# Moving the flags of rows without a matching key from VectorE to GpSimd

## The chip, the cores and the metric

One core of a Trainium2 chip runs the whole program. A core has five engines with a queue each: TensorE (PE, with its weight loads as PEld), VectorE (DVE), ScalarE (ACT), GpSimd (POOL) and SyncE (SP), which issues most of the DMA transfers. An engine takes its instructions in the order in which the program issues them, and waits on semaphores for what other engines produce. The metric is the device time of one execution in microseconds; lower is better. TensorE's granted clock is full speed in the whole profile.

## The reference

Bucketed attention over 2 x 8 heads, 768 positions and 64 dimensions, followed by two dense layers with gates. Only the first part matters here:

```python
q_bucket, k_bucket = ...            # 6 sign bits of a projection, as a number
mask = q_bucket[:, :, :, None] == k_bucket[:, :, None, :]
scores = scale * np.matmul(q, k.transpose(0, 1, 3, 2))
scores = np.where(mask, scores, -1000000000.0)
scores = scores - np.max(scores, axis=-1, keepdims=True)
attn = np.exp(scores)
attn = attn / (np.sum(attn, axis=-1, keepdims=True) + 1e-09)
return np.matmul(attn, v).astype(np.float32)
```

A query whose bucket holds no key has all its scores at -1e9; after the maximum is subtracted they are all 0, and its attention is 1/768 for every key. These rows need a flag.

## The kernel before, in words

The attention works on 8 pairs of heads (`NPAIR`), and on each pair in 12 units: one head, 128 queries, all 768 keys. So there are 96 units, numbered 0 to 95. Scores are made with their sign turned, and a large constant is added where the buckets differ: with `BIG` = 2^30, a masked score is at least `BIG / 2`. The softmax's maximum is therefore a minimum here, and a row without a matching key is one whose minimum is at least `BIG / 2`.

A unit n goes through these steps:

- `emit_S` (TensorE, L742): four passes into PSUM: high part of keys by high part of queries, high by low, low by high (`KL`, "kl"), and the bucket bits (`BK`, `BQ`).
- `emit_min` (VectorE, L751): the minimum of each row, into slot 0 of the group's statistics tile "st".
- `emit_exp` (ScalarE, L756): the exponential into tile "p", with the row's sum into slot 1.
- `emit_stats` (VectorE, L764 to L767): for a group of up to four units at once, four small operations that make the factor (slot 3) and the summand (slot 4) of each row.
- `emit_norm` (GpSimd, L772): p times factor plus summand, in place, one instruction for each unit.
- `emit_T` and `emit_tevac`: twelve transposes on TensorE (L784), then copies of the transposed halves out of PSUM into "pt" by ScalarE (L496) and VectorE (L497).
- `emit_pv` (TensorE, L797): attention times values.

The order is written out by hand. `attention_step(n)` takes units n and n + 1 together (n is even) and issues, beside their scores, minima and exponentials, the transposes of units n - 7 and n - 6 and the products of units n - 12 and n - 11. Groups are units 0 to 2, 3 to 6, 7 to 10, and so on to 91 to 94, and 95 alone. From n = 14 on, a step with n % 4 == 2 ends with `stats_norms` for units n - 3 to n: the four statistics on VectorE, then four normalisations on GpSimd.

In the same steps the next pair is prepared (`prep`, by s = (n // 2) % 6). At s = 1 GpSimd makes the high parts of keys and queries (`prep_kh`, `prep_qh`, L500), and, for the fourth pair on, the scaled bits (`prep_scale`, L526). At s = 5 it makes the low part of the keys (`prep_k_lo`, L549), and SyncE then issues the loads of the pair after that (L464, L473), into the buffer that the low part was read from. Both are issued ahead of the step's `stats_norms`:

```python
if nxt and s == 1:
    prep(nxt, s)
if live and n % 4 == 2 and n > 10:
    if nxt and s == 5:
        prep(nxt, s)
    stats_norms(range(n - 3, n + 1))
```

The first two pairs have an order of their own (`late_prep`, `mid_prep`): statistics of units 0 to 2 come after step 4, those of units 3 to 6 after step 6. VectorE and ScalarE also prepare the weights of the dense layers during the attention (`w_slot`, `w_parts`, for instance L155, L164, L147). After the last step the rest is written out: transposes of the last units, statistics and normalisation of unit 95, products, and the first dense matmuls (`emit_h`, L295; `emit_y`, L348). From there to the end, some 530 us, the dense layers run.

Of the kernel before, what the change touches and what calls it, by code (L numbers as in the profile page):

```python
# [8 lines left out]
F32 = mybir.dt.float32  # L9
# [3 lines left out]
ALU = mybir.AluOpType  # L13
AX = mybir.AxisListType
BIG = float(2 ** 30)
# [5 lines left out]
def bucket_attention_two_moe_kernel(  # L21
# [17 lines left out]
    B, H, D, S = q.shape  # L39
# [38 lines left out]
    V, A, G, P = nc.vector, nc.scalar, nc.gpsimd, nc.tensor  # L78
# [35 lines left out]
    units = [(k, i) for k in range(2 * NF) for i in range(2)]  # L114
# [156 lines left out]
    with tc.manual_schedule():  # L271
# [164 lines left out]
        with ExitStack() as actx:  # L436
# [8 lines left out]
            def big2(nm):  # L445
                return [big.tile([128, 2, HALF], F32R, name=f"{nm}{i}") for i in range(2)]

            KH, KL, BK = big2("kh"), big2("kl"), big2("bk")
# [62 lines left out]
            def prep_kh(p):  # L511
                scaled(KH[p % 2], raw_t[p, "k"], 1.0)
# [121 lines left out]
            for h in range(2):  # L634
                G.tensor_scalar(out=BK[1][:, h], in0=BK[1][:, h].bitcast(F32), scalar1=c8[:, 5 + 2 * h:6 + 2 * h],
                                scalar2=1.0, op0=ALU.add, op1=ALU.mult)
# [17 lines left out]
            def first_bq(out, ps, less):  # L654
                V.tensor_scalar(out=out, in0=ps, scalar1=0.0, scalar2=less, op0=ALU.is_gt, op1=ALU.subtract)
# [29 lines left out]

            first_z = []

            def mid_prep(n):
                if n == 2:
                    first_z.append(z_all("t1", q0[0][:, halves[1]], odd=q0[1][:, halves[1]]))  # L690

            def late_prep(n):
                if n == 0:
                    first_bk(1, "t1")
                    first_bq(bx[:, halves[0]], z_all("t0", q0[1][:, halves[0]]), cvec0)
                    first_q(1, 1)
                elif n == 2:
                    first_bq(BQ[0][:, halves[1]], first_z.pop(), cvec0)
                    prep_kh(1)
                    prep_qh(1)  # L700
                    rest_of(QL[1][0][:, halves[0]], raw_t[1, "q"][:, halves[0]].bitcast(F32),
                            QH[1][0][:, halves[0]], halves[0])
                    swap(QL[1], halves[0])
                elif n == 4:
                    prep_bit(1)
                    prep_scale(1)
                    stats_norms(range(3))
                    prep_bits(1, (0, 1, 3))
                elif n == 6:
                    load_v(0)  # L710
                    emit_stats(1, range(3, 7))
                    for x in (3, 4, 5):
                        emit_norm(x)
                    prep_k_lo(1, 0)
                    emit_norm(6)
                    prep_k_lo(1, 1)
                    G.tensor_scalar(out=BK[0][:, 1], in0=BK[1][:, 1].bitcast(F32), scalar1=1.0, scalar2=1.0,
                                    op0=ALU.mult, op1=ALU.mult)


            L = 7
            NU = NPAIR * 12
            s_t, p_t, st_t, pt_t, tb_t, pv_t = {}, {}, {}, {}, {}, {}
# [34 lines left out]
                p_t[n] = pt  # L758


            def emit_stats(b, units):
                mine = slice(units[0] + 1 - 4 * b, units[-1] + 2 - 4 * b)
                least, total, inv, mul, add = (st_t[b][:, i, mine] for i in range(5))
                V.tensor_scalar(out=add, in0=least, scalar1=BIG / 2, scalar2=1.0 / S, op0=ALU.is_ge, op1=ALU.mult)  # L764
                V.tensor_scalar(out=inv, in0=total, scalar1=1e-9, scalar2=None, op0=ALU.add)
                V.reciprocal(out=inv, in_=inv)
                V.scalar_tensor_tensor(out=mul, in0=least, scalar=BIG / 2, in1=inv, op0=ALU.is_lt, op1=ALU.mult)  # L767

            def emit_norm(n):
                b, i = divmod(n + 1, 4)  # L770
                st = st_t[b]
                G.tensor_scalar(out=p_t[n], in0=p_t[n], scalar1=st[:, 3, i:i + 1], scalar2=st[:, 4, i:i + 1],  # L772
                                op0=ALU.mult, op1=ALU.add)
# [38 lines left out]
            def emit_pv_hi(gi):  # L812
                for hi, lo, src in x_parts(gi):
                    A.copy(hi, src)
# [6 lines left out]


            def stats_norms(units):
                emit_stats((units[0] + 1) // 4, units)
                for n in units:
                    emit_norm(n)

            def attention_step(n, w_act=(), w_dve=(), mid=lambda: None, between=lambda: None):
                u = n - L
                m = n - 12  # L830
                live = n < NU
                have = [0 <= u + k < NU for k in range(2)]
                if n == NU:
                    stats_norms(range(NU - 1, NU))
                def first_T():
                    if have[0]:
                        emit_T(u)
                        emit_tevac(u, 0, acp)
                        if n < 14:
                            emit_min(n)  # L840
                        emit_tevac(u, 1, acp if live and n >= 14 else vcp)
                        if n == 12:
                            stats_norms(range(7, 11))

                if n >= 14:
                    first_T()
                if n == 0:
                    for i, passes in ((0, range(3)), (1, range(1)), (0, range(3, 4)), (1, range(1, 4))):
                        emit_S(i, passes)
                elif live:  # L850
                    emit_S(n)
                    if n < 14:
                        first_T()
                    emit_S(n + 1)
                mid()
                if have[1]:
                    emit_T(u + 1)
                s = n // 2 % 6
                nxt = n // 12 + 1 if live and n // 12 + 1 < NPAIR else None
                if nxt and s == (2 if nxt < 3 else 1):  # L860
                    prep_z(nxt)
                for k in (m, m + 1):
                    if 0 <= k < NU:
                        emit_pv(k // 6, k % 6)
                out_gi = m // 6 if m + 2 == NU else m // 6 - 1 if m >= 6 and m % 6 == 0 else None
                if out_gi is not None:
                    emit_pv_hi(out_gi)
                    if live and out_gi % 2 == 0:
                        out_gi = None
                if live and s == 4 and m > 0:  # L870
                    out_gi = m // 6 - 1
                for part in w_act:
                    part()
                early = live and have[1]
                if early and n >= 14:
                    emit_tevac(u + 1, 0, acp)
                if live:
                    if n >= 14 or not have[0]:
                        emit_min(n)
                    emit_exp(n)  # L880
                    emit_min(n + 1)
                if early and n < 14:
                    emit_tevac(u + 1, 0, acp)
                between()
                if have[1]:
                    emit_tevac(u + 1, 1, acp if n == 6 else vcp)
                if have[1] and not early:
                    emit_tevac(u + 1, 0, acp)
                if n + 2 < NU:
                    emit_exp(n + 1)  # L890
                if n == 12:
                    prep_q_lo(1, 1)
                    swap(QL[1], halves[1])
# [6 lines that stand above are left out]
                elif nxt and s == 5:  # L900
                    prep(nxt, s)
                if nxt and s not in (1, 5):
                    prep(nxt, s)
                if out_gi is not None:
                    emit_pv_lo(out_gi)
                    if out_gi % 2 == 1 and out_gi // 2 + 2 < NPAIR:
                        load_v(out_gi // 2 + 2)
                for part in w_dve:
                    part()
# [15 lines left out]
            for n in range(0, NU, 2):  # L925
                if n == 12:
                    two_banks()
                attention_step(n, *w_at.get(n // 2, ((), ())),
                               mid=lambda: mid_prep(n))
# [16 lines left out]
            def late_pv(gi):  # L946
                for j in range(NJ):
                    emit_pv(gi, j)
# [8 lines left out]
            emit_exp(NU - 1)  # L957
            late_T(NU - 6, "s0")
            late_pv(last - 1)
            stats_norms(range(NU - 1, NU))  # L960
            late_out(last - 2)
            qctx.close()
            more = ctx.enter_context(tc.tile_pool(name="more", bufs=1, reuse_waits="tile"))
# [75 lines left out]
```

## Time and profile before

| | |
|---|---|
| median of 3 runs | 729.79 us (729.0 to 729.97) |
| profiled execution | 729.23 us, its span 727.5 us |
| TensorE busy | 721.1 us (99%), 4726 matmuls |
| VectorE busy | 483.1 us (66%), 908 instructions |
| ScalarE busy | 422.9 us (58%), 808 instructions |
| GpSimd busy | 136.0 us (19%), 139 instructions |
| attention stage, about | 0 to 197 us |

Times in the trace count from the start of the span. A busy share is an average over stages: GpSimd works only in the attention stage, and there it is busy for most of the time. An instruction's idle time is put down to what released it; where several semaphores are waited for, to the one that came last.

### The profile page before, as it was taken

The page shows a single profiled execution, that of the slowest core. Times are in us where ns is not written, and L with a number is a line of the kernel's source. Part 1 is how long each engine was busy: PE and PEld are TensorE (multiplying, and loading weights), DVE is VectorE, ACT ScalarE, POOL GpSimd, SP SyncE. Part 2 cuts the span into 40 slices and gives each one's busy share as a digit, 9 for nine tenths or more (in the row PEclk, how much of TensorE's full clock was granted, in tenths as well). Part 3 has the DMA queues.
Part 4 walks back from the last instruction along what each step waited for, and adds up shares of the span by engine and source line. Part 5 has one row for each costly group of instructions (what it writes and reads, how often), then busy time and mean ns, then how long its engine had stood idle before and what let it go on. Part 6 is the DMA issues. An engine that isn't in the chain of part 4 may idle for free.

```text
span 727.5 us, 12377 instructions
## 1 busy us (share of the span) xinstructions
PE 721.1 (99%) x4726; PEld 571.8 (79%) x4726; DVE 483.1 (66%) x908; ACT 422.9 (58%) x808; POOL 136.0 (19%) x139
## 2 busy tenths in 40 slices
PE   8999999999999999999999999999999999999998
PEld 5776776767778888888888888888888888888886
DVE  8989889888899969696582386584665556121212
ACT  6898888889787857674462264553444444222221
POOL 6876676665500000000000000000000000000000
PEclk9999999999999999999999999999999999999999
DMA  4433434341043322232120002122112100010101
GB/s 137 147 120 85 138 109 126 101 147 65 2 145 117 124 108 89 85 117 75 41 87 29 1 29 84 37 83 84 62 58 81 64 30 1 0 59 1 58 1 58
DMA packets 20274, 54.29 MB, mean 75 GB/s; under 512 B 3008, under 2 KB 7032, under 8 KB 20216
## 3 DMA queue, kind: packets, MB, share of 16 engines
q1 hardware_dynamic: 19912, 53.28, 22.1%
q8 instruction: 37, 0.61, 0.3%
q10 hardware_dynamic: 304, 0.23, 0.1%
q14 instruction: 21, 0.17, 0.1%
HBM read 43.39 MB, written 3.15 MB: 64 GB/s over the span
## 4 chain that ended last, share of the span: by engine, by line
PE 98%; DVE 2%; ACT 0%; issue 0%; DVEq 0%
PE s L348 34%; PE t L295 18%; PE pv L295 10%; PE s L742 9%; PE m L295 7%; PE t L784 5%; PE pv L797 5%; PE m L797 5%; DVE st L751 1%; PE m L348 1%; PE m L486 1%; PE t L348 1%; PE t L645 1%; PE t L570 1%; PE s L295 0%; DVE pt L497 0%
## 5 line engine op out<-in xcount | busy, mean ns | idle before, releaser
L327 DVE TENSOR_TENSOR gl<-gr,gh 128x512 fp32r<-128x512 f32 x96 | 66.1, 689 | 116.6 <-PE s L348 86.0
L772 POOL TENSOR_SCALAR p<-p,st 128x768 f32<-128x768 f32 x96 | 96.9, 1024 | 45.8 <-DVE st L767 37.1
L751 DVE TENSOR_REDUCE st<-s 128x1 f32<-128x768 f32 x96 | 87.6, 951 | 16.7 <-PE s L742 16.2
L323 ACT CAST gh<-gr 128x512 fp32r<-128x512 f32 x96 | 59.6, 621 | 61.9 <-PE s L348 37.2
L756 ACT ACTIVATE p<-s,st 128x768 f32<-128x768 f32 x96 | 86.2, 908 | 1.4 <-DVE st L751 1.2
L295 PE MATMUL t<-xh,wil 128*128 128x512 f32 x196 | 76.2, 389 | 0.0
L295 PE MATMUL t<-xh,wih 128*128 128x512 f32 x196 | 76.2, 389 | 0.0
L295 PE MATMUL t<-xl,wih 128*128 128x512 f32 x196 | 76.2, 389 | 0.0
L496 ACT COPY pt<-t 128x384 f32<-128x384 f32 x134 | 60.5, 491 | 25.3 <-PE t L784 24.6
L348 PE MATMUL s<-gh,woh 128*128 128x512 f32 x192 | 74.8, 390 | 0.0
L348 PE MATMUL s<-gh,wol 128*128 128x512 f32 x192 | 74.7, 389 | 0.0
L784 PEld LDWEIGHTS t<-ident,p 64*128 64x128 f32 x1104 | 47.4, 138 | 29.8 <-issue 15.5
L348 PE MATMUL s<-wol,gh 128*128 128x512 f32 (+1 forms) x178 | 69.0, 388 | 0.0
L348 PE MATMUL s<-woh,gh 128*128 128x512 f32 (+1 forms) x178 | 69.0, 388 | 0.0
L155 DVE SCALAR_TENSOR_TENSOR raw<-raw 128x512 uint32<-128x512 uint32 x64 | 46.1, 720 | 16.9 <-ACT raw L151 16.9
L784 PE MATMUL t<-ident,p 64*128 64x64 f32 x1104 | 54.1, 227 | 1.5 <-POOL p L772 1.2
L348 PE MATMUL s<-gl,woh 128*128 128x512 f32 x192 | 51.5, 389 | 0.0
L348 PE MATMUL s<-woh,gl 128*128 128x512 f32 (+1 forms) x178 | 49.6, 388 | 0.0
L173 ACT ACTIVATE raw<-raw 128x512 f32<-128x512 uint32 x64 | 43.0, 673 | 1.1 <-DVE raw L155 1.1
L315 ACT ACTIVATE gr<-t 128x512 f32<-128x512 f32 x24 | 14.4, 598 | 49.7 <-PE t L295 46.9
L151 ACT ACTIVATE raw<-raw 128x512 uint32<-128x512 uint32 x64 | 43.0, 672 | 0.0
L295 PEld LDWEIGHTS t<-xh,wih 128*128 128x128 f32 x196 | 36.8, 188 | 7.7
(161 smaller groups left out, 1513.1 us busy)
## 6 DMA issues: line engine op xcount, KB each, us to landing
raw<-in_moe_w_in_dram SPq DMA_DIRECT2D x32, 512.0 KB
raw<-in_moe_w_out_dram SPq DMA_DIRECT2D x32, 512.0 KB
vn<-in_v_dram SPq DMA_DIRECT2D x8, 384.0 KB
out_dram<-yp SPq DMA_DIRECT2D x11, 256.0 KB
k<-in_k_dram SPq DMA_DIRECT2D x14, 192.0 KB
q<-in_q_dram SPq DMA_DIRECT2D x7, 384.0 KB
qh<-qh SPq DMA_DIRECT2D x14, 192.0 KB
ql<-ql SPq DMA_DIRECT2D x12, 192.0 KB
```

Source lines behind the costliest of these rows:

```text
L155: V.scalar_tensor_tensor(out=low, in0=high, scalar=23, in1=low, op0=ALU.logical_shift_left, op1=ALU.bitwise_or)
L295: P.matmul(ps, lhsT=w[:, cs], rhs=x[t][:, c, :], start=(n == 0), stop=(n == 3 * KB - 1))
L323: A.copy(new_g(i)[0], gr_t[i])
L327: V.tensor_tensor(out=gl, in0=gr_t.pop(i), in1=gh.bitcast(F32), op=ALU.subtract)
L348: P.matmul(ys[d][:, part_cs] if len(ys) == 4 else ys[d // 2][:, d % 2, :], lhsT=w, rhs=g[:, part_cs], start=((fresh or j == 0) and part == ...
L496: acp = lambda o, i: A.copy(o, i)
L742: P.matmul(ps[:, r, :HALF], lhsT=w[rows, qs], rhs=bx[rows, halves[1]] if own and x == 3 else m[rows, h], start=(x == 0), stop=(x == 3))
L751: V.tensor_reduce(out=st_t[b][:, 0, i:i + 1], in_=s_t[n][:, :, :HALF], op=ALU.min, axis=AX.XY)
L756: A.activation(out=pt, in_=s_t.pop(n)[:, :, :HALF], func=AF.Exp, scale=-1.0, bias=st_t[b][:, 0, i:i + 1], accum_out=st_t[b][:, 1, i:i + 1])
L772: G.tensor_scalar(out=p_t[n], in0=p_t[n], scalar1=st[:, 3, i:i + 1], scalar2=st[:, 4, i:i + 1], op0=ALU.mult, op1=ALU.add)
L784: P.transpose(tb_t[n][r][:, j * 64:(j + 1) * 64], src[rows, j // 3, j % 3 * 128:(j % 3 + 1) * 128], ident[rows, rows])
L797: P.matmul(pv_t[gi][64 * h:64 * h + 64, :HALF], lhsT=vn_t[p][:, h, j, :], rhs=pt_t[gi, h][:, j, :], start=(j == 0), stop=(j == NJ - 1), ti ...
```

## The change

The flags are made by GpSimd with two small operations per group (`emit_flags`): the summand (1/768 or 0), and a number "more" that is 1e-9 for an ordinary row and about 1.3e30 for a flagged one. VectorE adds "more" to the row's sum and takes the reciprocal; a flagged row's factor is then so small that its products vanish beside the summand. The flags are issued in `between(n)`, which is called right after the minimum of unit n + 1, ahead of the copies out of PSUM and of `prep`. At the start of the stage some normalisations and one copy of the bits (`BK[0]`) change places too.

```diff
+            def between(n):
+                if n == 6:
+                    emit_norm(1)
+                    emit_flags(range(3, 7))
+                    emit_norm(2)
+                elif n == 10:
+                    emit_flags(range(7, 11))
+                    G.tensor_scalar(out=BK[0][:, 1], in0=BK[1][:, 1].bitcast(F32), scalar1=1.0, scalar2=1.0,
+                                    op0=ALU.mult, op1=ALU.mult)
+                elif n % 4 == 2 and n > 10:
+                    emit_flags(range(n - 3, n + 1))
...
                 elif n == 2:
                     first_bq(BQ[0][:, halves[1]], first_z.pop(), cvec0)
+                    emit_flags(range(3))
                     prep_kh(1)
                     prep_qh(1)
...
-                    stats_norms(range(3))
+                    emit_stats(range(3))
+                    emit_norm(0)
                     prep_bits(1, (0, 1, 3))
                 elif n == 6:
                     load_v(0)
-                    emit_stats(1, range(3, 7))
+                    emit_stats(range(3, 7))
                     for x in (3, 4, 5):
                         emit_norm(x)
                     prep_k_lo(1, 0)
                     emit_norm(6)
                     prep_k_lo(1, 1)
-                    G.tensor_scalar(out=BK[0][:, 1], in0=BK[1][:, 1].bitcast(F32), scalar1=1.0, scalar2=1.0,
-                                    op0=ALU.mult, op1=ALU.mult)
...
-            def emit_stats(b, units):
-                mine = slice(units[0] + 1 - 4 * b, units[-1] + 2 - 4 * b)
-                least, total, inv, mul, add = (st_t[b][:, i, mine] for i in range(5))
-                V.tensor_scalar(out=add, in0=least, scalar1=BIG / 2, scalar2=1.0 / S, op0=ALU.is_ge, op1=ALU.mult)
-                V.tensor_scalar(out=inv, in0=total, scalar1=1e-9, scalar2=None, op0=ALU.add)
-                V.reciprocal(out=inv, in_=inv)
-                V.scalar_tensor_tensor(out=mul, in0=least, scalar=BIG / 2, in1=inv, op0=ALU.is_lt, op1=ALU.mult)
+            def group(units):
+                b = (units[0] + 1) // 4
+                return [st_t[b][:, i, units[0] + 1 - 4 * b:units[-1] + 2 - 4 * b] for i in range(5)]
+
+            def emit_flags(units):
+                least, total, more, mul, add = group(units)
+                G.tensor_scalar(out=add, in0=least, scalar1=BIG / 2, scalar2=1.0 / S, op0=ALU.is_ge, op1=ALU.mult)
+                G.tensor_scalar(out=more, in0=add, scalar1=1e33, scalar2=1e-9, op0=ALU.mult, op1=ALU.add)
+
+            def emit_stats(units):
+                least, total, more, mul, add = group(units)
+                V.tensor_tensor(out=mul, in0=total, in1=more, op=ALU.add)
+                V.reciprocal(out=mul, in_=mul)
...
                     emit_min(n + 1)
                 if early and n < 14:
                     emit_tevac(u + 1, 0, acp)
-                between()
+                if live:
+                    between(n)
...
             late_T(NU - 6, "s0")
             late_pv(last - 1)
+            emit_flags(range(NU - 1, NU))
             stats_norms(range(NU - 1, NU))
             late_out(last - 2)
```

`stats_norms` calls the new `emit_stats`, without the group's number. The statistics at n == `NU` in `attention_step`, which no step reached, are gone.

## Rows read from the trace of the kernel before

**Rows 1.** Windows: the middle of the attention stage, busy time by engine (instructions).
```profile
29.00:190.00 161.00, 161.00 (x2034) 114.41 (x2030) 142.00 (x268) 137.81 (x323) 109.76 (x107) 1.00 0.37 111
```

**Rows 2.** The chain that ended last, start of the attention stage (start, duration).
```profile
16.49 1.73 DVE st L751 x2
...
19.52 0.87 DVE st L751
...
26.61 0.58 PE t L784 x11
```

**Rows 3.** Timeline of VectorE, the same stretch (start, duration, instruction).
```profile
15.54 0.47 DVE L764 TENSOR_SCALAR st<-st 128x3 f32<-128x3 f32 x1
...
18.14 0.44 DVE L764 TENSOR_SCALAR st<-st 128x4 f32<-128x4 f32 x1
...
18.89 0.64 DVE L767 SCALAR_TENSOR_TENSOR st<-st 128x4 f32<-128x4 f32 x1
```

**Rows 4.** Timeline of GpSimd, the same stretch (start, duration, instruction).
```profile
13.26 0.83 POOL L500 TENSOR_SCALAR kh<-k 128x768 fp32r<-128x768 f32 x1
...
14.97 1.02 POOL L660 TENSOR_TENSOR ql<-qn,qh 128x384 fp32r<-128x384 f32 x1
16.60 5.95 POOL L772 TENSOR_SCALAR p<-p,st 128x768 f32<-128x768 f32 x6 [0.62 <-DVE st L767]
```

**Rows 5.** Groups on VectorE: two statistics, one weight operation (busy, mean ns).
```profile
L155 DVE SCALAR_TENSOR_TENSOR raw<-raw 128x512 uint32<-128x512 uint32 x64 | 46.1, 720 | 16.9 <-ACT raw L151 16.9
...
L766 DVE RECIPROCAL st<-st 128x4 f32<-128x4 f32 x23 | 4.1, 178 | 0.8
L764 DVE TENSOR_SCALAR st<-st 128x4 f32<-128x4 f32 x23 | 4.0, 172 | 0.0
```

**Rows 6.** Groups on GpSimd: two that bound a small operation.
```profile
L717 POOL TENSOR_SCALAR bk<-bk 128x384 fp32r<-128x384 f32 x1 | 0.5, 529 | 0.0
...
L1016 POOL MEMSET const-float32-1.0<- 128x1 f32 x1 | 0.1, 98 | 0.0
```

**Rows 7.** Timeline of VectorE around units 46 and 47.
```profile
91.81 1.42 DVE L155 SCALAR_TENSOR_TENSOR raw<-raw 128x512 uint32<-128x512 uint32 x1
93.14 1.81 DVE L751 TENSOR_REDUCE st<-s 128x1 f32<-128x768 f32 x2
```

**Rows 8.** Timeline of GpSimd, units 22 (first row) and 46.
```profile
45.58 1.85 POOL L549 TENSOR_TENSOR kl<-k,kh 128x768 fp32r<-128x768 f32 x1
...
92.64 2.27 POOL L549 TENSOR_TENSOR kl<-k,kh 128x768 fp32r<-128x768 f32 x1
```

**Rows 9.** Timeline of TensorE around units 46 to 48.
```profile
92.54 0.33 PE L742 MATMUL s<-bk,bq 64*128 64x384 f32 x2
...
96.24 0.40 PE L742 MATMUL s<-kl,qh 64*128 64x384 f32 x2
```

**Rows 10.** Timeline of SyncE: the next pair's loads.
```profile
94.93 1.35 SPq L464 DMA_DIRECT2D k<-in_k_dram  x2
```

**Rows 11.** Windows: the same loads in flight, DMA share and GB/s at the end.
```profile
96.30:99.40 3.10, 3.10 (x38) 2.08 (x37) 2.56 (x6) 2.62 (x8) 3.10 (x4) 1.00 0.86 258
```

**Rows 12.** Timeline of TensorE: the bits of the next pair.
```profile
101.57 0.51 PE L486 MATMUL m<-q,pz 128*32 128x384 f32 x1
```

**Rows 13.** Timeline of GpSimd, end of the attention stage.
```profile
189.91 5.52 POOL L772 TENSOR_SCALAR p<-p,st 128x768 f32<-128x768 f32 x5 [3.59 <-DVE st L767]
```

**Rows 14.** Timeline of VectorE, end of the attention stage.
```profile
192.75 0.55 DVE L818 TENSOR_TENSOR xl<-m,xh 128x384 fp32r<-128x384 f32 x1
193.22 1.11 DVE L155 SCALAR_TENSOR_TENSOR raw<-raw 128x512 uint32<-128x512 uint32 x1
...
195.10 0.56 DVE L497 COPY pt<-t 128x384 f32<-128x384 f32 x1 [0.43 <-PE t L784]
195.96 1.02 DVE L497 COPY pt<-s 128x384 f32<-128x384 f32 x2 [0.30 <-ACT pt L496]
```

**Rows 15.** Timeline of TensorE, end of the attention stage.
```profile
196.66 0.59 PE L784 MATMUL s<-ident,p 64*128 64x64 f32 x12 [0.36 <-DVE pt L497]
```

More of the change, by code (lines that the diff above doesn't have):

```diff
@@ L823, in stats_norms, with attention_step @@
             def stats_norms(units):
-                emit_stats((units[0] + 1) // 4, units)
+                emit_stats(units)
                 for n in units:
                     emit_norm(n)
-            def attention_step(n, w_act=(), w_dve=(), mid=lambda: None, between=lambda: None):
+            def attention_step(n, w_act=(), w_dve=(), mid=lambda: None):
                 u = n - L
@@ L832, in attention_step @@
                 have = [0 <= u + k < NU for k in range(2)]
-                if n == NU:
-                    stats_norms(range(NU - 1, NU))
                 def first_T():
```

## The prediction

> **What bounds the kernel now.** I read the page first, then windows over its stages, then the chain of waits, and last the timelines of the places where the change puts a new wait. In the middle of the attention stage TensorE is busy for all of 161.00 us, VectorE for 142.00, ScalarE for 137.81 and GpSimd for 109.76 [rows 1]. So there VectorE has some 12% to spare, and freeing it buys nothing: a step gets longer only if TensorE is made to wait, and shorter not at all. The stage's start is different. Between 13.25 and 26.6 us the chain of waits runs mostly through VectorE (minima at 16.49 and 19.52) and passes to TensorE for good with the transposes at 26.61 [rows 2]. There a microsecond of VectorE is nearly a microsecond of the end. After the attention stage the change touches nothing.
>
> **The change part by part.** The arithmetic that leaves VectorE is two of four small operations per group, 25 groups. One costs 172 ns, the reciprocal 178 [rows 5]. Two such are 0.35 us a group (23 of four units, and one each of three and of one), some 8.8 us in all; where TensorE sets the pace they are worth nothing, because the idle of VectorE takes them. What counts is three new waits: GpSimd's flags wait for the minima, what stands behind the flags in GpSimd's queue waits with them, and VectorE's addition waits for GpSimd.
>
> The price f of a pair of flag operations is not in the trace. GpSimd needs 98 ns to fill one element and 529 for a scalar operation over 384 [rows 6]; over 768 it needs 830 [rows 4]. The straight line through the last two leaves 0.23 us at no elements. Two, the second reading the first, make f about 0.5 us. Bounds: 0.2 (two fills of one element) and 1.06 (two of 384). The line is nearest, so I take 0.5.
>
> How a small VectorE operation fares beside GpSimd is in the trace. L764 at 15.54 takes 0.47 us and ends at 16.01, where GpSimd's ql operation ends (14.97 + 1.02) [rows 3, 4]. The six normalisations from 16.60 take 5.95, 0.99 each, so their borders are at 17.59, 18.58 and 19.57; L764 ends at 18.58 and L767 (18.89 + 0.64) at 19.53 [rows 3, 4]. A VectorE operation of this kind that comes while GpSimd works ends with GpSimd's instruction. I price the new addition like those.
>
> The Trainium skill (SBUF — State Buffer, Who interferes with whom) speaks against the change here: a VectorE instruction with two SBUF inputs shares a read interface with GpSimd, and whichever starts later waits for the whole instruction of the other. The new addition has two SBUF inputs (totals and "more"). The borders above agree. Without that rule, at 0.16 us for the addition, the first term below would be about 0.1 instead of 1.2.
>
> *First term, the stage's start.* The flags of units 0 to 2 go ahead of kh, qh and ql in GpSimd's queue, which run from 13.26 to 15.99 without a gap worth counting [rows 4]. With f they end at 16.49. VectorE's addition comes at 15.54, into ql, and ends with it; with the reciprocal (0.4 for both) the group is done at 16.85. Then VectorE takes two minima, 1.73 [rows 2], until 18.6. GpSimd normalises units 0 and 1 from 16.95 to 18.9, makes the flags of units 3 to 6 until 19.4, and starts on unit 2 at once. VectorE's addition, which needs those flags, comes just behind that start, ends with it at 20.4, and the next minimum starts at 20.8, against 19.52 before [rows 2]: 1.3 later. If the first addition slips in ahead of ql, it is 1.0. I take 1.2. Bounds: a GpSimd that is never in the way would let the minimum start at 15.62 + 0.4 + 1.73 + 0.4, near 18.15, a gain of 1.4; f of 1.06 gives a loss of 2.4. The third early group has its flags long before it is due.
>
> *Second term, the end of each pair.* In the last group of a pair, GpSimd's k_lo, the low part of the next pair's keys, stood right behind the previous normalisations and ended at 94.91 [rows 8]. TensorE uses it at 96.24 [rows 9], 1.3 us later. Now the flags stand ahead of it, and they wait for the minimum of unit 46. The scores of that unit end at 92.54 + 0.33 [rows 9]; one minimum is 0.95 (two take 1.81), so it is there at 93.85, if the weight operation before it, 1.42 long beside a mean of 0.72 [rows 5, 7], is through by then, and at 94.1 if not. Add 0.1 to reach GpSimd, f of 0.5, k_lo of 1.85, its time when nothing interferes (at unit 22; the 2.27 at unit 46 overlaps that slowed weight operation [rows 7, 8]), and 0.1 to reach TensorE: 2.55 after the minimum. TensorE gives it 96.24 - 93.85 = 2.39. It waits 0.15 to 0.4. There are six such places (units 22, 34, 46, 58, 70, 82): 6 x 0.2 = 1.2 us. Bounds: f of 0.2 makes it nothing; f of 1.06 makes 6 x 0.7 = 4.3.
>
> The next pair's loads also wait for k_lo: they are issued at 94.93 [rows 10], and move 258 GB/s from 96.3 to 99.4, 800 KB, which is the keys and queries [rows 11]. 1.5 us later they end near 100.9, ahead of TensorE's use at 101.57 [rows 12]. I take nothing; if landing takes 1 us more than the data, the places cost another 0.3 each.
>
> In the other groups the flags have their minimum long before the exponentials that the addition needs anyway, and GpSimd idles. Where kh and qh stand behind the flags, they move some 2 us and the normalisations 0.3; the transposes take them over 2 us later. VectorE's additions behind GpSimd cost it up to 1 us there, which its idle covers.
>
> *Third term, the end of the stage.* Unit 95's statistics used to run as soon as VectorE reached them, ending at 192.75 [rows 14], while GpSimd still normalised units 91 to 94. Now VectorE's addition needs flags that stand behind those four in GpSimd's queue. They end at about 189.91 + 4 x 0.98 = 193.8 [rows 13], some 0.25 earlier after a shorter group; with f, 0.1 to cross and 0.4 for the two operations VectorE goes on at 194.55, 1.8 late. Queued behind it are L818, L155 and its clamp, then the PSUM copies at 195.10 and 195.96, ahead of which it idled 0.43 and 0.30 [rows 14]. So the copies come 1.8 - 0.73 = 1.1 later. TensorE's last transposes already wait for one of them, at 196.66 [rows 15]. I take 1.0; bounds 0.6 and 1.5, by f.
>
> *Sum.* 1.2 + 1.2 + 1.0 = 3.4 us more. The profiled execution took 729.23 (span 727.5, 1.7 around it), which is 0.56 under the median of the three runs and within their range; on their mean, 729.6, the forecast is 733.0.
>
> **The rivals.** *Only one wait bites.* If VectorE's addition isn't held up and k_lo ends in time, the third term remains, 1.0 or a little less: 730.6, no measurable change (within 0.2%, 1.5 us, is about what a measurement of this kernel can't tell from no change). For it: k_lo misses by only some 0.15. Against it: the borders in [rows 3, 4].
>
> *Dear flags.* f of about 1 us: 2.4 + 4.3 + 1.5 = 8.2, so 737.8. Against it: the 98 ns fill.
>
> *Keys in time, the rest as forecast.* 1.2 + 1.0: 731.8, still slower.
>
> *The start gains.* VectorE's chain from 15.54 is shortened by what leaves it, and GpSimd is never in its way: 1.4 less, 728.2, if the flags of units 3 to 6 are done when VectorE has its minima, near 17.75. It decides for faster only if the last group's flags are early too. Against it: two normalisations stand ahead of those flags, and GpSimd's queue was full until 15.99 [rows 4].
>
> **How the numbers follow.** Forecast, all three terms, 732.2 to 734.5: 0.50. Keys in time: 0.10. Dear flags: 0.08. Only one wait: 0.25. The start gains: 0.07. Slower by over 0.2% is the first three and a little of the fourth, 0.69; within it 0.25; faster 0.06. The range for 8 in 10 runs from just under the one-wait case, 730.2, to 736.2, where f is near 0.8.
>
> **What the profile after would show.** At the start, the minimum of unit 8 at 20.8 instead of 19.5, and an addition on VectorE that ends with a normalisation. At the six places, k_lo beginning after the minimum, not behind the normalisation, and TensorE's key-low matmuls late by 0.2. At the end, VectorE's last addition waiting on GpSimd until 194, and the last transposes near 197.7. Flags of 0.1 us each, an addition that runs beside GpSimd, or a TensorE without idle at the pairs' ends would make it wrong.

## The result, and the profile after

The changed kernel takes 735.71 us, median of 5 runs (735.11 to 737.55), beside 729.79 for the kernel before (729.0 to 729.97, 5 runs there). It is slower by 5.9 us going by the two medians, and by 6.5 going by the measured ratio, 1.0089 with a 95% interval of 1.0077 to 1.0100. The forecast was 3.2 to 3.4. The profiled execution took 735.71, its span is 733.9, 6.4 longer than before.

The page, busy time by engine. VectorE has 50 instructions fewer and is busy for only 3.1 us less; GpSimd has 50 more, 8.0 us:

```profile
PE 724.7 (99%) x4726; PEld 572.9 (78%) x4726; DVE 480.0 (65%) x858; ACT 422.7 (58%) x808; POOL 144.0 (20%) x189
```

The groups of GpSimd and of VectorE behind that difference (out<-in, count, busy, mean ns, idle before). The two flag operations of a group take 0.23 and 0.20 us. The addition, an operation on four elements per row, takes 478 ns on average, so what replaced 17 us on VectorE costs 15. The six k_lo operations take 11.0 us, 2.2 less than before:

```profile
L549 POOL TENSOR_TENSOR kl<-k,kh 128x768 fp32r<-128x768 f32 x6 | 11.0, 1828 | 0.5
...
L778 POOL TENSOR_SCALAR st<-st 128x4 f32<-128x4 f32 x23 | 5.4, 233 | 28.8 <-DVE st L762 28.6
L779 POOL TENSOR_SCALAR st<-st 128x4 f32<-128x4 f32 x23 | 4.6, 200 | 2.0
```

```profile
L783 DVE TENSOR_TENSOR st<-st 128x4 f32<-128x4 f32 x23 | 11.0, 478 | 5.9 <-ACT p L767 4.0 <-POOL st L779 1.8
...
L784 DVE RECIPROCAL st<-st 128x4 f32<-128x4 f32 x23 | 4.1, 178 | 0.8
```

**The middle of the stage.** TensorE, without idle there before [rows 1], now has some:

```profile
29.00:194.00 165.00, 163.19 (x2039) 114.53 (x2036) 140.80 (x226) 138.38 (x325) 116.97 (x149) 1.00 0.37 109
```

The chain that ended last shows where, at unit 46 (start, duration, what released what). The minimum ends at 95.18; the two flag operations with the gaps around them take 0.68, to k_lo's start at 95.86; k_lo ends at 97.70; TensorE's key-low matmuls begin with it. In the kernel before the low keys had been ready 1.3 us ahead [rows 8, 9]. The bits matmuls of the next pair begin 5.6 us after k_lo's end, where it had been 6.7 before [rows 8, 12], and take 0.97 in the chain instead of 0.78:

```profile
93.12 1.18 DVE raw L155
94.31 0.88 DVE st L762
95.18 0.08 issue
95.26 0.24 POOL st L778
95.50 0.08 issue
95.58 0.20 POOL st L779
95.78 0.08 issue
95.86 1.84 POOL kl L549
97.70 0.04 issue
97.74 1.34 PE s L753 x10
...
103.33 0.97 PE m L486 x8
```

The same chain at unit 70: k_lo, then the issue of the keys' two loads, the landing of the queries 5.8 us after k_lo, then the bits matmuls:

```profile
144.07 1.83 POOL kl L549
...
145.93 0.67 SPq L464
...
146.63 0.64 SPq L464
...
147.32 4.42 DMA q<-in_q_dram
...
151.88 0.97 PE m L486 x8
```

Each step's first key-low matmul starts later by some amount than the same matmul in the kernel before. Followed through the steps, this lag gives a ledger of the profiled execution, and a loss shows as an increase that stays:

| where | TensorE falls back by, us | forecast |
|---|---|---|
| start of the stage, by step 12 | 0.12 | 1.2 |
| key-low matmuls at six pair ends, and the step after each | 2.1 (0.42, 0.32, 0.34, 0.35, 0.36, 0.35) | 1.2 |
| bits matmuls, at units 38, 50 and 74 | 1.3 (0.41, 0.30, 0.62) | 0 |
| unit 86 | 0.2 | |
| end of the stage, last transposes | 1.2 | 1.0 |
| first dense matmuls, at half clock | 1.6 | not named |
| all | 6.5 | 3.4 |

The line for the start is no firmer than about 0.3 us. The first scores began 0.29 us earlier here than in the trace of the kernel before. In the run below that puts the start back as it was (the last one), the lag at the same step is -0.34. What costs the 0.2 at unit 86 was not looked for.

**The end of the stage.** TensorE stands still for 1.33 us ahead of the last but one unit's transposes, where it had waited 0.36 for the last [rows 15]. The wait goes back through VectorE's queue to its last addition, at 198.10, as forecast:

```profile
199.47 0.24 PE L801 MATMUL t<-ident,p 64*128 64x64 f32 x1
201.04 0.58 PE L801 MATMUL t<-ident,p 64*128 64x64 f32 x11 [1.33 <-DVE pt L497]
...
202.11 0.50 PE L295 MATMUL s<-xh,wih 128*128 128x512 f32 x1
```

```profile
198.10 0.16 DVE L783 TENSOR_TENSOR st<-st 128x1 f32<-128x1 f32 x1 [2.27 <-POOL st L779]
...
198.38 0.54 DVE L835 TENSOR_TENSOR xl<-m,xh 128x384 fp32r<-128x384 f32 x1
198.83 1.35 DVE L155 SCALAR_TENSOR_TENSOR raw<-raw 128x512 uint32<-128x512 uint32 x1
200.11 0.41 DVE L147 TENSOR_SCALAR wih<-wih 128x512 f32<-128x512 f32 x1
200.45 0.54 DVE L497 COPY pt<-t 128x384 f32<-128x384 f32 x1
```

The windows from 200 us on (length, busy by engine, granted clock third from the end): after that pause the granted clock of TensorE falls to 0.50, 1.2 GHz instead of 2.4, and the first 12 dense matmuls take 4.5 us instead of 2.9:

```profile
200.00:202.00 2.00, 0.96 (x23) 0.88 (x23) 2.00 (x6) 0.52 (x2) 0.00 (x0) 1.00 0.00 0
202.00:204.00 2.00, 2.00 (x12) 1.60 (x9) 1.61 (x4) 1.87 (x5) 0.00 (x0) 0.74 0.00 0
204.00:206.00 2.00, 2.00 (x6) 1.52 (x6) 1.97 (x5) 1.08 (x2) 0.00 (x0) 0.50 0.00 0
206.00:208.00 2.00, 2.00 (x10) 1.62 (x9) 1.81 (x5) 1.24 (x3) 0.00 (x0) 0.91 0.80 262
```

### The profile page after: what moved, and what is told of

Same layout as the page of the kernel before. It is cut to its first block, busy times and chain, and to the rows that moved or that the text cites. A ratio compares the mean times of both kernels' runs of the same rounds, so it can differ in the third digit from the quotient of the medians.

```text
span 733.9 us, 12391 instructions
## 1 busy us (share of the span) xinstructions
PE 724.7 (99%) x4726; PEld 572.9 (78%) x4726; DVE 480.0 (65%) x858; ACT 422.7 (58%) x808; POOL 144.0 (20%) x189
## 4 chain that ended last, share of the span: by engine, by line
PE 88%; DVE 5%; POOL 3%; DMA 1%; SPq 1%; issue 1%; ACT 0%; POOLq 0%; DVEq 0%; ACTq 0%
PE s L348 34%; PE t L295 18%; PE pv L295 10%; PE m L295 7%; PE s L753 6%; PE pv L814 4%; PE t L801 4%; DVE st L762 3%; PE m L814 3%; POOL kl L549 2%; DMA q<-in_q_dram 1%; PE m L348 1%; PE m L486 1%; POOL p L789 1%; DVE pt L497 1%
## 5 line engine op out<-in xcount | busy, mean ns | idle before, releaser
L767 ACT ACTIVATE p<-s,st 128x768 f32<-128x768 f32 x96 | 86.1, 905 | 0.9 <-DVE st L762 0.6
```

The source lines that it names most:

```text
L767: A.activation(out=pt, in_=s_t.pop(n)[:, :, :HALF], func=AF.Exp, scale=-1.0, bias=st_t[b][:, 0, i:i + 1], accum_out=st_t[b][:, 1, i:i + 1])
```

## The experiments

The theory of the waits says that the loss lies in what stands behind the flags in GpSimd's queue (k_lo, and the loads behind it) and in the flags that stand behind other work (unit 95). The main rival is that 50 more small operations on GpSimd cost by themselves, by holding up VectorE or by being issued. Ratios are to the kernel before on the same chip, with their 95% intervals.

### Flags behind k_lo

```diff
-                elif n % 4 == 2 and n > 10:
+                elif n % 4 == 2 and n > 10 and (n // 2 % 6 != 5 or n // 12 + 1 >= NPAIR):
                     emit_flags(range(n - 3, n + 1))
...
                     if nxt and s == 5:
                         prep(nxt, s)
+                        emit_flags(range(n - 3, n + 1))
                     stats_norms(range(n - 3, n + 1))
```

> The changed kernel, but in the six groups that end a pair (units 22, 34, 46, 58, 70, 82) the flags are issued behind k_lo instead of ahead of it. Theory of the waits: TensorE's late starts there (about 2.2 us by the lateness of its key-low matmuls) and the late bits matmuls (1.4 us at three of five places, behind the loads that wait for k_lo) go away together, 3.5 us less: near 732.2. Rival, that 50 more small operations on GpSimd cost by themselves, through the port shared with VectorE or by their issue: no gain beyond 0.5, near 735.5.

Measured: 729.98, ratio 1.0013 (1.0003 to 1.0022). More went than was expected, 5.5 us by the ratios instead of 3.5. In the trace the six late starts and the bits' are gone. At five of the six pairs' ends TensorE is even 0.1 to 0.2 us earlier than before; there VectorE's weight operation takes 1.26 us instead of 1.42, and its copies come some 0.1 sooner, which is the likely reason. And the first dense matmuls take 2.9 us: behind the pause at the end the clock doesn't fall in this execution. The waits of TensorE (us, times, longest) hold nothing of GpSimd's k_lo or the loads; the wait at the end of the stage is still there:

```profile
PE t L801 <- DVE pt L497: 1.5, 2, 1.3
PE t L801 <- POOL p L789: 1.3, 1, 1.3
```

The first row is mostly the 1.3 us pause near the end of the stage. The second is the first transposes of all, which wait for the first normalisation in the kernel before as well.

### Unit 95's flags early

```diff
                 if live:
                     between(n)
+                    if n == NU - 2:
+                        emit_flags(range(NU - 1, NU))
...
             late_pv(last - 1)
-            emit_flags(range(NU - 1, NU))
             stats_norms(range(NU - 1, NU))
```

> The changed kernel, but the flags of unit 95 are issued in step 94, ahead of the normalisations of units 91 to 94. Theory of the waits: VectorE's last addition no longer stands behind those, TensorE's pause of 1.3 us before its last transposes goes, and with it the 3.3 us at half clock that followed it: 1.2 + 1.6 = 2.8 less, near 732.9, with a granted clock of 1.00 all through. Rival, that the clock falls in the profiled execution for another reason: 1.2 less, near 734.5, with the stretch at 0.5 still there.

Measured: 733.30, ratio 1.0053 (1.0038 to 1.0068); the granted clock is 1.00 or 0.999 in all four runs, and the first dense matmuls take 2.9 us. The pairs' ends still lose what they lost.

### Both

> Both moves together. Theory of the waits: 735.7 - 3.5 - 2.8 = 729.4, the time of the kernel before within what can be told; all of the loss was in the places where the flags stand, none in making them. Rival, cost of the operations themselves: above 731.5.

Measured: 728.77, ratio 0.9994 (0.9985 to 1.0004). All of the loss is gone with two moves, while all 50 operations stay on GpSimd. So they have no net cost of their own that could be told, and that rival is out. By the ratios the moves take away 5.5 and 2.6 us alone and 6.9 together. They don't add up, since in both profiled executions the fall of the clock at the end is missing as well. TensorE's waits are down to those that the kernel before has too, and one of 0.2 us:

```profile
PE t L801 <- POOL p L789: 1.3, 1, 1.3
...
PE s L801 <- DVE pt L497: 0.4, 1, 0.4
PE t L801 <- DVE pt L497: 0.2, 1, 0.2
```

### Queries loaded ahead of keys

```diff
                     raw_t[p, "k"] = qk_p.tile([128, 2, HALF], F32R, tag="k", name="k")
-                    load_k(p, raw_t[p, "k"])
+                    if p < 3:
+                        load_k(p, raw_t[p, "k"])
                     raw_t[p, "q"] = qk_p.tile([128, S], F32R, tag="q", name="q")
                     nc.sync.dma_start(...)
+                    if p >= 3:
+                        load_k(p, raw_t[p, "k"])
```

> The changed kernel, but from the fourth pair on the queries are loaded ahead of the keys. The buffer of the queries is free long before k_lo ends; that of the keys is not. If the bits matmuls were late because 800 KB of loads started late, only half of it is late now: those 1.4 us go, TensorE's late starts on the key-low matmuls stay: near 734.3. Rival, that these matmuls waited for VectorE or for their PSUM bank: unchanged, near 735.7.

Measured: 733.24, ratio 1.0055 (1.0040 to 1.0070), 2.5 us less than the changed kernel (whose median was 735.71, and 735.72 in the runs below). SyncE now issues the queries at 91.93, 6.4 us ahead of the keys:

```profile
91.93 0.56 SPq L474 DMA_DIRECT2D q<-in_q_dram  x1
98.31 1.36 SPq L464 DMA_DIRECT2D k<-in_k_dram  x2
```

The bits matmuls wait at no place, the key-low matmuls at the same places as in the changed kernel:

```profile
PE t L804 <- DVE pt L500: 1.6, 2, 1.3
PE t L804 <- POOL p L792: 1.4, 1, 1.4
...
PE s L756 <- POOL kl L552: 0.9, 5, 0.2
```

So the bits were late behind the loads, also where the trace of the changed kernel names VectorE (0.2 us). In the ledger of this run the bits cost nothing. The median gained 2.5, a microsecond more than the 1.3 of the changed kernel's ledger line. That line varies, from 1.2 to 2.1 in the six profiled executions whose late loads stand behind k_lo with the queries last; the rest isn't settled.

### Each part alone, on the kernel before

First the changed kernel once more, beside the same runs of the kernel before:

> The changed kernel once more, beside the same runs of the kernel before as the three below, so that parts and whole stand on one chip. Both theories: ratio 1.007 to 1.010; where its granted clock is 1.00, some 0.5 us less than where it is 0.998.

Measured: 735.72, ratio 1.0088 (1.0073 to 1.0103), the clock 0.998 in all four. In this profiled execution the fall of the clock lies not at the end, though the pause of 1.3 us is there, but between 20 and 24 us. The same holds for the run with the queries first, where it begins at 19.65. The windows of this run:

```profile
20.00:22.00 2.00, 1.96 (x23) 1.68 (x24) 1.65 (x4) 1.84 (x5) 1.90 (x3) 0.65 0.13 35
22.00:24.00 2.00, 2.00 (x24) 2.00 (x24) 1.42 (x2) 1.75 (x5) 2.00 (x3) 0.50 0.11 29
```

So a granted clock of 0.998 over a whole execution doesn't tell where the clock fell.

Only unit 95's flags:

```diff
+            least, total, more, mul, add = (st_t[NU // 4][:, i, :1] for i in range(5))
+            G.tensor_scalar(out=add, in0=least, scalar1=BIG / 2, scalar2=1.0 / S, op0=ALU.is_ge, op1=ALU.mult)
+            G.tensor_scalar(out=more, in0=add, scalar1=1e33, scalar2=1e-9, op0=ALU.mult, op1=ALU.add)
+            V.tensor_tensor(out=mul, in0=total, in1=more, op=ALU.add)
+            V.reciprocal(out=mul, in_=mul)
+            emit_norm(NU - 1)
-            stats_norms(range(NU - 1, NU))
```

> The kernel before with one part of the change: unit 95's flags on GpSimd, behind the normalisations of units 91 to 94, and its addition and reciprocal on VectorE. Theory of the waits: TensorE's pause ahead of its last transposes, 1.2 us more, and up to 1.6 on top in executions where the clock falls after it: ratio 1.0015 to 1.004. Rival, that this wait only costs when TensorE is already late: 1.000.

Measured: 730.95, ratio 1.0022 (1.0012 to 1.0031). In the ledger TensorE falls back by 1.2 before the first dense matmuls and by 1.6 more in them. Three of the ten runs have a granted clock of 0.998: 732.10, 732.27 and 732.31. The seven at 1.00 take 730.47 to 731.21, with a middle of 730.81. The difference is 1.5 us, near the 1.6 of the ledger. That the fall lies behind the pause is shown for the first of the three, which was profiled; for the other two it isn't known. These are the windows of the first; TensorE is busy for 0.61 of the 2 us ahead of the fall:

```profile
196.00:198.00 2.00, 0.61 (x13) 0.54 (x15) 2.00 (x5) 0.44 (x2) 0.00 (x0) 1.00 0.00 0
198.00:200.00 2.00, 2.00 (x16) 1.65 (x17) 1.62 (x5) 1.87 (x4) 0.00 (x0) 0.63 0.00 0
200.00:202.00 2.00, 2.00 (x7) 1.54 (x6) 1.97 (x4) 1.41 (x3) 0.00 (x0) 0.51 0.00 0
```

Only a wait ahead of k_lo:

```diff
                     if nxt and s == 5:
+                        least = st_t[(n + 1) // 4][:, 0, :]
+                        G.tensor_scalar(out=probe[:, 0], in0=least, scalar1=BIG / 2, scalar2=1.0 / S, op0=ALU.is_ge,
+                                        op1=ALU.mult)
+                        G.tensor_scalar(out=probe[:, 1], in0=probe[:, 0], scalar1=1e33, scalar2=1e-9, op0=ALU.mult,
+                                        op1=ALU.add)
                         prep(nxt, s)
```

> The kernel before with two small GpSimd operations of the flags' form added ahead of k_lo in the six groups that end a pair; they read the same minima, their results are used by nobody, and VectorE keeps its own four. Theory of the waits: key-low matmuls late by 0.35 at each of six places, 2.1 us, and the bits matmuls late behind the loads, 1.4 to 2.1: 3.5 to 4.2 more, ratio 1.005 to 1.006. Rival, that the loss is in VectorE's additions waiting for GpSimd: 1.000 to 1.001, since no VectorE instruction waits for these.

Measured: 734.72, ratio 1.0072 (1.0057 to 1.0087): 5.2 us from twelve operations whose results nobody reads. The key-low matmuls lose 3.0 in the ledger, the bits 1.7. No addition waits for GpSimd here, so the rival that the loss lies in those waits is out. The key-low part is 0.8 larger than in the changed kernel. In the trace VectorE's weight operation takes 1.42 us here, as in the kernel before, and 1.26 in the changed kernel, and the minimum behind it comes that much later; the normalisations beside it end later too.

### Filling the pause at the end

```diff
+                if n == NU - 2:
+                    fill = bank("m")
+                    for _ in range(6):
+                        P.matmul(fill[:, :128], lhsT=ident, rhs=ident, start=True, stop=True)
                 late_T(n, side)
```

> The changed kernel with six idle matmuls of 128x128, 0.24 us each, ahead of the last but one unit's transposes, into a PSUM bank that is free there; they fill TensorE's pause of 1.3 us and nobody uses their result. Theory, that the clock falls because TensorE stands still there: no stretch at 1.2 GHz after it, the first dense matmuls take 2.9 us and not 4.5, and the median is 0.5 to 1.5 lower than the changed kernel's. Rival, that the clock falls for a reason elsewhere: the stretch stays and the time is the same.

Measured: 734.61, ratio 1.0074 (1.0059 to 1.0089), 1.1 less than the changed kernel beside it. The granted clock is 1.00 or 0.999 in all four runs, and in the windows where it had been 0.5:

```profile
200.00:202.00 2.00, 2.00 (x26) 1.81 (x27) 2.00 (x5) 0.50 (x2) 0.00 (x0) 1.00 0.00 0
202.00:204.00 2.00, 2.00 (x19) 1.67 (x20) 1.62 (x4) 1.91 (x4) 0.00 (x0) 1.00 0.00 0
204.00:206.00 2.00, 2.00 (x11) 1.65 (x9) 1.96 (x4) 1.88 (x4) 0.00 (x0) 1.00 0.00 0
```

With matmuls that compute nothing TensorE is busy through the pause, and no fall follows. The waiting itself, 1.1 us in the ledger, they leave. This fits the theory that the clock falls because TensorE stands still there, but doesn't show it. The changed kernel beside it has its profiled fall at 20 to 24 us, which the fill can't reach, and the two intervals overlap, so the 1.1 can't be put down to the fill.

All the traces together say this much. The pause of 1.3 to 1.4 us stands unfilled in six of the changed versions' profiled executions. Behind it the clock falls in two (the changed kernel's first, and unit 95's flags alone) and stays up in four. In the seven executions where this pause is missing or filled, the kernel before among them, it falls at the end in none. Over all runs, 14 of the 34 of those six versions have a granted clock of 0.998 or less, and 2 of the 97 of the others, but where the clock fell is known for the profiled ones alone. So the pause is the likely cause of the fall behind it, not the shown one, and what decides between the two and the four stays open.

### The addition at the start

```diff
+                    V.tensor_scalar(out=probe, in0=group(range(3, 7))[2], scalar1=1.0, scalar2=None, op0=ALU.mult)
                     emit_stats(range(3, 7))
```

> The changed kernel with one more small VectorE operation ahead of the addition of units 3 to 6; it reads the same flags and its result is used by nobody. In the changed kernel that addition took 0.16 us, between GpSimd's second flag operation and its next normalisation, which then began 0.09 behind the flags. Theory of the shared port: the extra operation takes that gap, the addition comes 0.2 later, meets the running normalisation and ends with it, 0.6 to 1.0 long, and the minimum of unit 8 starts 0.8 to 1.0 later than 3.1 us behind the flags' first operation or so. Rival, that a small addition isn't held up at all by a normalisation: 0.16 again, the minimum 0.2 later.

One run, 734.90. The extra operation began at 19.49 and the addition at 19.57, for 0.17 us; the normalisation began at 19.56. The addition came only 0.01 behind, and it wasn't held up. This doesn't decide between the two: the delay was too short to put the addition well into the normalisation.

### Two versions beyond both moves

In the first, the flags of units 3 to 6 go ahead of the normalisations of units 1 and 2:

```diff
-                    emit_norm(1)
                     emit_flags(range(3, 7))
+                    emit_norm(1)
                     emit_norm(2)
```

> Both moves, and at the start of the stage the flags of units 3 to 6 stand ahead of the normalisations of units 1 and 2 instead of between them. VectorE's addition waits 1 to 1.7 us for them in the runs so far. Theory: the wait goes, the minimum of unit 8 starts 0.5 earlier, and 0.2 to 0.4 of it reaches TensorE: ratio 0.9985 to 0.9995. Rival, that the normalisation of unit 1, now 0.6 later, holds up its transposes by as much: 1.000.

Measured: 729.01, ratio 0.9994 (0.9985 to 1.0003), the same as both moves alone. The wait is shorter and the minimum of unit 8 began 0.6 earlier than with both moves alone, but the times don't tell theory and rival apart. Two of the eleven runs have a granted clock of 0.998, 730.16 and 730.23, in a version without the pause of 1.3 us at the end; where the clock fell in them isn't known.

In the second, the first three groups are as in the kernel before:

```diff
             def between(n):
-                if n == 6:
-                    ...
-                elif n == 10:
-                    ...
-                elif n % 4 == 2 and n > 10 and (n // 2 % 6 != 5 or n // 12 + 1 >= NPAIR):
+                if n % 4 == 2 and n > 10 and (n // 2 % 6 != 5 or n // 12 + 1 >= NPAIR):
                     emit_flags(range(n - 3, n + 1))
...
             def emit_stats(units):
                 least, total, more, mul, add = group(units)
+                if units[0] < 11:
+                    V.tensor_scalar(out=add, in0=least, scalar1=BIG / 2, scalar2=1.0 / S, op0=ALU.is_ge, op1=ALU.mult)
+                    V.tensor_scalar(out=more, in0=total, scalar1=1e-9, scalar2=None, op0=ALU.add)
+                    V.reciprocal(out=more, in_=more)
+                    V.scalar_tensor_tensor(out=mul, in0=least, scalar=BIG / 2, in1=more, op0=ALU.is_lt, op1=ALU.mult)
+                    return
```

> Both moves, and the first three groups (units 0 to 10) have their four operations on VectorE and their order as in the kernel before; the other groups have their flags on GpSimd, behind k_lo where a pair ends. Theory: the start is that of the kernel before, the pairs' ends gain about 0.1 each because VectorE's copies there come earlier, the end is that of the kernel before: 0.5 to 0.7 less than before, ratio 0.9990 to 0.9995. Rival, that no part of it can be told from the kernel before: 1.000.

Measured: 728.76, ratio 0.9991 (0.9982 to 1.0000). It is 0.6 us under the kernel before, at the edge of what can be told, and not to be told from the versions with both moves. So the changed start costs nothing that can be measured either. In the ledger the pairs' ends gain some 0.7 together, as with the flags behind k_lo. At most that is what the freed VectorE is worth here.

## Why the prediction was half right

The direction was right, and two of the three places that it named (the pairs' ends and the stage's end) lost time by the mechanism that it gave. The size came out at about half. Two steps failed: the late loads were put at nothing and cost 1.3 us, and the clock's fall behind the pause, 1.6 in the profiled execution, was in no term. Of the terms in the sum, the pairs' ends were too small (1.2 for 2.1) and the start too large (1.2 for 0.1).

*What bounds the kernel.* Right. VectorE's time bought next to nothing in the middle of the stage, 0.7 us at most; TensorE's waits, and its clock behind one of them, made the difference.

*The price of the flags.* 0.5 us was forecast; from the first operation to the start of what follows it is 0.60 in the chain. The straight line through two sizes gave 0.23 for an operation, and 0.23 and 0.20 came. What it lacked is the 0.08 behind each.

*First term, the start: mis-sized, 1.2 forecast, 0.1 in the profiled execution.* The flow was as described, but neither addition was held up. The first came at 15.49 and was over at 15.64; ql, into which the prediction had put it, began at 15.67. The second began at 19.29, 0.06 ahead of the next normalisation; the prediction had put it just behind that start. The gain of 1.4 that the prediction gave for this case didn't come either, because the second addition had waited 1.68 for the flags, which stand behind two normalisations:

```profile
15.49 0.15 DVE L783 TENSOR_TENSOR st<-st 128x3 f32<-128x3 f32 x1
...
19.29 0.16 DVE L783 TENSOR_TENSOR st<-st 128x4 f32<-128x4 f32 x1 [1.68 <-POOL st L779]
...
48.50 0.96 DVE L783 TENSOR_TENSOR st<-st 128x4 f32<-128x4 f32 x1 [0.24 <-ACT p L767]
```

```profile
15.67 1.01 POOL L660 TENSOR_TENSOR ql<-qn,qh 128x384 fp32r<-128x384 f32 x1
...
19.05 0.20 POOL L779 TENSOR_SCALAR st<-st 128x4 f32<-128x4 f32 x1
19.35 3.91 POOL L789 TENSOR_SCALAR p<-p,st 128x768 f32<-128x768 f32 x4
...
47.62 1.83 POOL L549 TENSOR_TENSOR kl<-k,kh 128x768 fp32r<-128x768 f32 x1
```

The mechanism that it used exists all the same, though of the two operations on whose borders it was based L764 has one input and only L767 has two. The addition at 48.50 takes 0.96 and ends with k_lo, at 49.46; the mean of 478 ns is made of such. In the executions in which the first scores begin later, at 6.8 us or after (6.5 or before in the others), the first addition does meet ql and takes 0.74 to 0.88 (five of the profiled executions, one of them of the changed kernel). The Trainium skill (SBUF — State Buffer, Who interferes with whom) says that a VectorE instruction with two SBUF inputs contends with a GpSimd instruction that reads SBUF, and calls what they share an exclusive lock. These rows agree: 0.96 and 0.74 to 0.88, beside 0.15 when nothing interferes. At the start the addition came first both times, by 0.18 and 0.06 us, and that decided.

*Second term, the pairs' ends: mechanism right, mis-sized, 1.2 forecast, 2.1 measured.* The chain from the minimum to TensorE was put at 2.55 and is 2.56 (95.18 to 97.74). What was short is the loss at each place: the forecast took 0.2 out of its own 0.15 to 0.4, where some 0.27 came, and it left out the step after, which loses 0.1 again.

*The loads: the step that failed.* "I take nothing" was 1.3 us. The bytes were priced by their rate (done near 100.9, which is 4.5 us after the k_lo that it expected), and the landing behind them was not. The landing comes 5.8 us after k_lo at unit 70, and 5.6 and 6.0 us after k_lo, TensorE's bits matmuls run late at units 50 and 74. The prediction named this case, 0.3 a place, and gave it no weight. That the loads are the cause is shown by loading the queries first, which leaves no loss at the bits, and by the two operations ahead of k_lo alone, which bring it back.

*Third term, the end: right, 1.0 forecast, 1.2 measured. What followed it failed.* The fall of TensorE's clock behind the pause, 1.6 us in this execution, was in no term. It doesn't follow in every execution, and what decides that stays open. The kernel before has a pause in the same place, of 0.36 us [rows 15], and its profile shows no fall.

*The sum.* 0.1 + 2.1 + 1.3 + 0.2 + 1.2 + 1.6 = 6.5 in the profiled execution, whose span is 6.4 longer. The 1.1 too much at the start covered part of what was left out; that 735.71 still lies in the stated range is owed to that, and so to luck. The two medians differ by less, 5.9, because the profiled execution of the kernel before, 729.23, is 0.56 under its median.

*The rivals.* "Dear flags", 737.8, came near in time and was wrong in cause: with both moves the operations cost nothing that can be told. "Keys in time", "only one wait" and "the start gains" didn't come: the keys were late at all six places.

## What to carry to other kernels

A small operation given to another engine costs what waits behind it in that engine's queue, and what waits for that in turn, DMA issues included; place it by when what stands behind it is due. Here two moves within the queue decided between 6.5 us of loss and none. A load's slack is to be read from the use back to the buffer's release, by landings in the trace, not by bytes over bandwidth. And where TensorE sets the pace, a pause of it should be priced twice: for itself, and for the clock, which fell behind it in two of six executions here.

## What was not expected of the hardware

Behind a pause of 1.3 to 1.4 us TensorE's granted clock was 0.50 for 3.4 us in two of six profiled executions, and the dense matmuls there took 1.6 us longer; with matmuls put into the pause the clock stayed at 1.00 or 0.999 in all four runs. The addition of two 4-element operands on VectorE took between 0.15 and 1.03 us in the changed kernel, and the long ones ended with the GpSimd instruction beside them.
